# Attention and two MLPs on one core: the work beside attention ordered by a model of the transfers, and casts moved to GpSimd

## The chip, the cores and the metric

One core of a Trainium2 chip runs the whole program. The metric is the device time of one execution in microseconds. Engines are named as in the profile: PE (TensorE), PEld (its weight loads), DVE (VectorE), ACT (ScalarE), POOL (GpSimd), SP (SyncE, which issues nearly all DMAs; its queue is SPq).

## What is computed

Sigmoid attention over 48 heads, then two MLPs, one behind the other, on the 1792 rows that come out:

```python
scores = q @ k.T / sqrt(64) - log(448)          # (4, 12, 448, 64) each, float32
x = (1 / (1 + exp(-scores))) @ v                # then heads side by side: (1792, 768)
h = x @ w_in;   x = where(h > 0, h, exp(min(h, 0)) - 1) @ w_out     # 768 -> 2048 -> 768
h = x @ w_in2;  return (h - tanh(h)) @ w_out2                       # 768 -> 2048 -> 768
```

The four weight matrices arrive as 8-byte floats and are narrowed to float32 on the chip.

## The kernel before

**Attention.** The 48 heads are 24 pairs. A pair's queries and keys are loaded (L222, and 64 rows of keys and values that don't fill a tile by L234 and L242), set side by side by POOL (L226), transposed by PE (L312 to L316) into one bank, copied out by DVE or ACT (`to_plain`, L327 and L329), and split in two parts for exact products: `hi` (L335, a cast) and `lo` (L339, what the cast lost). PE then makes scores (L358, L369), ACT the sigmoids (L375, L379), PE the products with the values (L387, L397), and DVE copies the result into the raw tiles R0a to R1b (`xdone`, L408). Two pairs are one round.

**Work beside attention.** While PE does attention, the other engines prepare what follows. Four blocks of the first `w_in` (L580, L582) and all 16 of the first `w_out` (L649, 768 KB each, tiles XB and XA) are loaded; each is narrowed in three steps, one on ACT (L598) and two on DVE (L601, L605); four sums of `w_out`'s parts are made (`p_sum`, L658) and all parts stored to DRAM (L663). From round six on the raw tiles are split into operands of the first product: `x_sum` (L759), `x_head` (L769, a cast on ACT), `x_rest` (L775, on DVE). There are 21 heads of operands for the first 1024 tokens and 21 for the other 768, each 128x512 or 128x384.

**The products.** Each MLP is two products, with Strassen's seven multiplications; PE runs them group by group (L803, then L958). One group of the first product is seven multiplications for each of the two parts of the tokens. ACT and DVE make its weights (L732, L735; POOL the sums of weights, L718) and take its results (L815 and on).

**What sets the order.** `Sched` holds operations with an engine, a cost, what they wait for and a rank. Attention alone is planned first (ranks from `PHASES`, a 12 us `ROUND` for two pairs); then everything is placed in one list by start time, and each engine's instructions stand in its queue in that order. An operation that isn't attention's is put on ACT or DVE only where it ends before the next planned one is due, give or take `GIVE`. A transfer counts as landed a fixed latency after its issue (2.5 to 12 us), however many are under way. Ranks of the side work are set by `fixed`: a block of `w_out` every 12 us.

```python
if k not in plan and planned.get(queue) and c[0] + ops[k][1] > plan[planned[queue][-1]] + late + GIVE:
    c = (10 ** 9,) + c[1:]
```

Of the kernel before, what the change touches and what calls it, by code (L numbers as in the profile page):

```python
# [16 lines left out]
class Sched:  # L17
# [3 lines left out]
    def __init__(self):  # L21
        self.ops, self.before, self.plan = {}, {}, {}
# [7 lines left out]

    def emit(self, only_plan=False):
        ops, plan, late = self.ops, self.plan, 0

        planned = {q: sorted((k for k in plan if ops[k][0] == q), key=plan.get, reverse=True) for q in ("ACT", "DVE")}
# [12 lines left out]
        while any(ready.values()):  # L47
            best = None
            for queue, keys in ready.items():
                t0 = free.get(queue, 0)  # L50
                for k, t in keys.items():
                    c = (max(t, t0), ops[k][4], str(k))
                    if k not in plan and planned.get(queue) and c[0] + ops[k][1] > plan[planned[queue][-1]] + late + GIVE:
                        c = (10 ** 9,) + c[1:]
                    if best is None or c < best[0]:
                        best = c, queue, k
# [8 lines left out]
            done[k] = free[queue] + ops[k][5]  # L65
            order.append((start, len(order), ops[k][2], k))
# [16 lines left out]
GIVE = 100  # L83

# [5 lines left out]
    "t": (2000 - ROUND, 2900 - ROUND), "plain": (2950 - ROUND, 4100 - ROUND), "hi": (4100 - ROUND, 5800 - ROUND), "lo": (4700 - ROUND, 6400 - ROUND),  # L90
    "side": (4500 - 2 * ROUND, 6000 - 2 * ROUND), "ldqk": (7000 - 3 * ROUND, 8500 - 3 * ROUND),
# [7 lines left out]
def kernel(  # L99
# [67 lines left out]
    with tc.manual_schedule():  # L167
# [7 lines left out]
        def attention():  # L175
# [31 lines left out]
            vrest = [vs_p.tile([128, NR, D], F32, name=f"vrest{i}") for i in range(2)]  # L207
# [31 lines left out]
            def ld_vr(g):  # L239
                for z in range(2):  # L240
                    for x in range(2):
                        nc.sync.dma_start(  # L242
                            out=vrest[g % 2][RS * z:RS * z + RS].rearrange("p (i x) d -> x p i d", x=2)[x],
                            in_=rests(1, g).rearrange("(i x h) p d -> x h p i d", x=2, h=2)[x, z ^ x],
                        )
# [27 lines left out]
            def loads(m):  # L273
# [12 lines left out]
                for x, key in enumerate(todo):  # L286
# [4 lines left out]
                    }.get(kind, [])  # L291
                    sch.op(key, "SP", {"ldkr": 2400, "ldvr": 2400}.get(kind, 600), lambda fn=fns[kind], args=args: fn(*args),
# [41 lines left out]
            def hi(n):  # L334
                nc.vector.tensor_copy(out=es[n % 2][:, :EW], in_=kq(n))  # L335
# [27 lines left out]
            def scores_rest(m):  # L363

                ps = buffer("sr", m)
                for x in range(2):
                    for j in range(2):
                        lanes, c = slice(64 * j, 64 * j + 64), 64 * (j ^ x)
# [1165 lines left out]
```

## Time and profile before

| | us |
|---|---|
| median of 3 runs (1009.24 to 1013.07) | 1009.57 |
| the profiled execution | 1009.88 |
| its span, first to last instruction | 1008.2 |
| PE busy, share of the span | 977.1, 97% |
| DVE busy | 780.1, 77% |
| ACT busy | 597.4, 59% |
| POOL busy | 112.1, 11% |

The rows below come from the profile's views: the page's busy times; the table of stretches (per stretch each engine's busy time with its count of instructions, PE's granted clock as a share of full speed, the share of DMA time and the GB/s moved); the timeline of one engine (start, duration, and in brackets the idle time before and what ended it); and groups of instructions by form (count, busy time, mean of one). A stretch from one L369 to another is a whole number of rounds.

### The profile page before, as it was taken

Reading aid. Unit: us, or ns where it says so; the run is one execution under the profiler, and the core shown is the slowest. Engines: PE = TensorE matmul, PEld = TensorE weight load, DVE = VectorE, ACT = ScalarE, POOL = GpSimd, SP = SyncE. Lnnn points to the kernel's source line nnn. Section 1 sums busy time; section 2 is a strip of 40 time slices with the busy share of each in tenths; the row PEclk is TensorE's granted clock in tenths of the full one; section 3 lists DMA queues with packets and bytes.
Section 4 is the critical chain, followed back from the end, with each engine's and each line's share of the span. In section 5 each row is a group of like instructions: output and inputs, shape, how many; then the busy total and the mean of one; then the engine's idle time right before and its main releaser. Section 6 shows DMA issues by size and latency. Waiting matters only on the chain.

```text
span 1008.2 us, 15604 instructions
## 1 busy us (share of the span) xinstructions
PE 977.1 (97%) x5306; PEld 844.7 (84%) x5306; DVE 780.1 (77%) x1143; ACT 597.4 (59%) x943; POOL 112.1 (11%) x110
## 2 busy tenths in 40 slices
PE   8989899689999999999999998999999999999998
PEld 5555455578888888888899997888888999999998
DVE  4879798977888888668887899777777788665673
ACT  4768578756666667665566654444444556446652
POOL 2211220202222220000000201111111000000000
PEclk9989899989999999999999999999999999999999
DMA  7899981066666679999984734455555894455442
GB/s 205 286 299 317 300 300 64 31 186 191 191 191 191 191 241 321 372 401 382 373 284 131 242 97 148 160 196 188 186 192 187 325 330 146 125 169 173 128 148 85
DMA packets 145087, 218.61 MB, mean 217 GB/s; under 512 B 21936, under 2 KB 103408, under 8 KB 144752
## 3 DMA queue, kind: packets, MB, share of 16 engines
q1 hardware_dynamic: 143744, 217.10, 64.6%
q8 instruction: 41, 0.67, 0.3%
q10 hardware_dynamic: 1264, 0.52, 0.2%
q14 instruction: 38, 0.31, 0.1%
HBM read 142.61 MB, written 74.97 MB: 216 GB/s over the span
## 4 chain that ended last, share of the span: by engine, by line
PE 90%; DMA 4%; DVE 2%; ACT 1%; issue 1%; SPq 0%; ACTq 0%; DVEq 0%
PE psa L803 13%; PE psd L803 12%; PE psx L803 10%; PE psu L958 7%; PE psv L958 7%; PE psw L958 7%; PE psa L958 6%; PE psb L958 6%; PE psb L803 5%; PE psy L958 5%; PE sps L358 4%; PE pvps L387 4%; PE psx L958 3%; PE psd L958 1%; DMA XB<-in_moe_w_out_dram 1%; DMA vl<-in_v_dram 1%
## 5 line engine op out<-in xcount | busy, mean ns | idle before, releaser
L930 ACT ACTIVATE XB<-t 128x384 fp32r<-128x384 f32 (+1 forms) x111 | 62.0, 562 | 37.5 <-PE psw L958 9.9
L718 POOL TENSOR_TENSOR second<-second 128x384 f32<-128x384 f32 x15 | 19.2, 1279 | 552.1 <-DMA t<-x_forms 213.5
L934 DVE TENSOR_TENSOR XB<-t,XB 128x384 fp32r<-128x384 f32 (+1 forms) x111 | 68.3, 626 | 11.4 <-ACT XB L930 11.1
L379 ACT ACTIVATE an<-sps,bias 128x896 f32<-128x896 f32 x72 | 68.6, 1008 | 3.7 <-PE pvps L387 2.0
L358 PE MATMUL sps<-e 64*128 64x448 f32 x432 | 55.1, 395 | 9.7 <-ACT ar L375 9.3
L358 PEld LDWEIGHTS sps<-e 64*128 64x128 f32 x432 | 40.3, 197 | 25.1 <-ACT ar L375 10.5
L930 ACT ACTIVATE XB<-spare 128x512 fp32r<-128x512 f32 (+1 forms) x72 | 41.1, 573 | 27.0 <-PE psw L958 11.2
L387 PE MATMUL pvps<-an,vl 128*64 128x448 f32 x288 | 56.8, 543 | 0.0
L803 PE MATMUL psa<-XB,W 128*128 128x512 f32 x192 | 54.6, 393 | 0.0
L934 DVE TENSOR_TENSOR XB<-spare,XB 128x512 fp32r<-128x512 f32 (+1 forms) x72 | 44.2, 622 | 8.0 <-ACT XB L930 7.7
L958 PE MATMUL psu<-XB,XB 128*128 128x384 f32 (+1 forms) x192 | 46.3, 348 | 0.0
L226 POOL COPY first<-raw_qk 128x384 f32<-128x384 f32 (+1 forms) x44 | 34.2, 798 | 109.1 <-DMA raw_qk<-in_k_dram 79.5
L958 PE MATMUL psv<-XB,XB 128*128 128x384 f32 (+1 forms) x192 | 46.1, 348 | 0.0
L958 PE MATMUL psw<-XB,XB 128*128 128x384 f32 (+1 forms) x192 | 46.1, 348 | 0.0
L387 PEld LDWEIGHTS pvps<-an,vl 128*64 128x64 f32 x288 | 19.6, 137 | 31.6 <-issue 29.1
L803 PEld LDWEIGHTS psa<-XB,W 128*128 128x128 f32 x192 | 36.4, 190 | 7.7
L832 ACT ACTIVATE spare<-t 128x512 f32<-128x512 f32 (+1 forms) x33 | 19.0, 579 | 36.9 <-DVE t L820 35.9
L718 POOL TENSOR_TENSOR first<-first,second 128x384 f32<-128x384 f32 x30 | 40.1, 1336 | 1.2
L803 PE MATMUL psd<-XB,W 128*128 128x512 f32 x144 | 37.0, 401 | 1.5 <-DVE W L735 1.3
L836 ACT ACTIVATE spare<-spare 128x512 f32<-128x512 f32 (+1 forms) x64 | 36.6, 572 | 0.7
L958 PE MATMUL psa<-XB,XB 128*128 128x384 f32 (+1 forms) x156 | 36.8, 347 | 0.0
L958 PE MATMUL psb<-XB,XB 128*128 128x384 f32 (+1 forms) x156 | 36.8, 347 | 0.0
(362 smaller groups left out, 2732.6 us busy)
## 6 DMA issues: line engine op xcount, KB each, us to landing
x_forms<-R1b SPq DMA_DIRECT2D x58, 256.0 KB, 2.0
first<-p_forms SPq DMA_DIRECT2D x36, 384.0 KB, 6.3
t<-x_forms SPq DMA_DIRECT2D x64, 192.0 KB, 2.9
t<-x_forms SPq DMA_DIRECT2D x47, 256.0 KB, 4.9
x_forms<-t SPq DMA_DIRECT2D x44, 256.0 KB, 2.0
x_forms<-R1b SPq DMA_DIRECT2D x58, 192.0 KB, 4.7
spare<-x_forms SPq DMA_DIRECT2D x36, 256.0 KB, 4.7
x_forms<-t SPq DMA_DIRECT2D x44, 192.0 KB, 3.4
```

Of the source, the lines that this page charges most:

```text
L226: nc.gpsimd.tensor_copy(out=(ql, kl)[w][:, n % NL].rearrange("p c (h d) -> p c h d", h=2), in_=x)
L358: nc.tensor.matmul(out=ps[:, j, :S], lhsT=e[lanes, EW * kz + u * 128:EW * kz + (u + 1) * 128], rhs=e[lanes, EW * qz + KW:EW * qz + EW], st ...
L379: nc.scalar.activation(out=a, in_=T.pop(("s", n, u))[:, :, :S], func=ACTF.Sigmoid, bias=bias, scale=scale)
L387: nc.tensor.matmul(out=T["o", m][D * j:D * j + D, j ^ x, :S], lhsT=vl[m % NVL][:, x, 3 * j + u], rhs=a[:, j], start=(u == 0), stop=False,)
L718: by.tensor_tensor(out=out, in0=x, in1=y, op=op)
L803: nc.tensor.matmul(out=ps, lhsT=w[wz][:, k0:k0 + 128], rhs=xs[xz][:, kk], start=(opens and n == 0), stop=(n == 3 * KH - 1), skip_group_che ...
L832: nc.scalar.activation(out=r, in_=h, func=ACTF.Tanh)
L836: nc.scalar.activation(out=r, in_=r, func=ACTF.Exp, scale=-1.0)
L930: nc.scalar.activation(out=at_place(og_place[i, s, p, j], 0, i)[:, :HW[s]], in_=T["graw", i, s, p, j], func=ACTF.Copy)
L934: nc.vector.tensor_tensor(out=lo, in0=T.pop(("graw", i, s, p, j)), in1=f(hi), op=ALU.subtract)
L958: nc.tensor.matmul(out=T["o2", tag], lhsT=lhsT, rhs=rhs, start=(p in OPENS and j == 0 and x == 0), stop=(j == NG - 1 and x == 2), skip_gro ...
```

## The change

It does six things.

1. `Sched.moves` gives each DMA a time on one pipe that all transfers share; a load counts as landed when the pipe has come to it.
2. `latest()` works out how late each planned operation of attention on ACT, DVE and POOL may start; side work may now delay it by 0.6 (`SLACK`) of that. POOL becomes a planned queue.
3. `hi` of pairs 2 to 23 moves from DVE to POOL, `x_head` of the first 1024 tokens (21 casts, 128x512) from ACT to POOL, and `x_sum` T3 and T4 of the other tokens (6 subtractions, 128x384) from DVE to POOL.
4. The heads of a pair keep their natural order: `pv` writes both heads of a pair to one bank, `scores_rest` and `pv_rest` use the four quarters of PE in another assignment, so the first `w_in` is loaded by one DMA a block where three stood.
5. The rows of `vrest` are laid out for that order, in four DMAs as before.
6. `fixed` paces the side work anew (a block of `w_out` every 14 us from the start, of `w_in` every 12 us), and `PHASES` moves `hi`, `lo`, `side` and `ldqk` a little.

```diff
-        planned = {q: sorted((k for k in plan if ops[k][0] == q), key=plan.get, reverse=True) for q in ("ACT", "DVE")}
+        planned = {q: sorted((k for k in plan if ops[k][0] == q), key=plan.get, reverse=True) for q in ("ACT", "DVE", "POOL")}
+        limit = self.latest() if plan else {}
...
-                    if k not in plan and planned.get(queue) and c[0] + ops[k][1] > plan[planned[queue][-1]] + late + GIVE:
+                    if k not in plan and planned.get(queue) and c[0] + ops[k][1] > limit[planned[queue][-1]] + late + GIVE:
...
+            if k in self.moves:
+                moved = max(moved, start + 1400) + self.moves[k]
+                done[k] = moved + 600
...
+    def latest(self):
...
+            if queue in ("PE", "SP"):
+                found[k] = plan[k]
+            else:
+                by = [found[u] - cost - latency for u in users[k]]
+                if queue in last:
+                    by.append(last[queue] - cost)
+                found[k] = max(plan[k], min(by, default=plan[k]))
+                last[queue] = found[k]
+        return {k: plan[k] + SLACK * (t - plan[k]) for k, t in found.items()}
...
-                nc.vector.tensor_copy(out=es[n % 2][:, :EW], in_=kq(n))
+                (nc.gpsimd if n > 1 else nc.vector).tensor_copy(out=es[n % 2][:, :EW], in_=kq(n))
...
-                        out=T["o", m][D * j:D * j + D, j ^ x, :S], lhsT=vl[m % NVL][:, x, 3 * j + u], rhs=a[:, j], start=(u == 0), stop=False,
+                        out=T["o", m][D * j:D * j + D, x, :S], lhsT=vl[m % NVL][:, x, 3 * j + u], rhs=a[:, j], start=(u == 0), stop=False,
...
-                        lanes = slice(64 * (j ^ x), 64 * (j ^ x) + 64)
+                        lanes = slice(64 * x, 64 * x + 64)
...
             def sums_on(i, s, x):
-                return "DVE"
+                return "POOL" if (i, s) == (0, 1) and x in ("T3","T4") else "DVE"
...
             def heads_on(i, s):
-                return "ACT"
+                return "ACT" if i or s else "POOL"
...
+                sch.moves["load", n] = 2700 if live and wide else 1100
...
-                    fixed[done] = 3 * CYCLE + n
+                    fixed[done] = n * ROUND
...
-                    fixed[k] = (2 * k[1] + 2) * CYCLE
+                    fixed[k] = 2 * k[1] * PACE
```

**What moves in the queues.** Line numbers differ between the two programs: L598 becomes L614, L375 L402, L379 L406, L649 L665, L663 L679, L222 L249, L718 L734.

On SP, around the load of the third block of `w_in` (R1a). Its narrowing on ACT stands in both programs right before the fifth `ar`. Before, from the loads of queries and keys of pairs 10 and 11 (`raw_qk`) to those of pairs 12 and 13:

```order
L222 DMA raw_qk<-in_q_dram 112x2x256
L663 DMA p_forms<-XB_71 128x4x384
L259 DMA vl_119<-in_v_dram 128x4x192
L663 DMA p_forms<-XB_71 128x384
L242 DMA vrest_117<-in_v_dram 64x2x64 x4
L580 DMA R1a<-in_moe_w_in_dram 64x6x256
L582 DMA R1a<-in_moe_w_in_dram 64x3x256 x2
L234 DMA krest_116<-in_k_dram 64x2x64 x4
L663 DMA p_forms<-XB_71 128x2x384
L222 DMA raw_qk<-in_k_dram 128x2x192
```

Now, up to the loads of pairs 10 and 11 and the values behind them:

```order
L665 DMA XB_71<-in_moe_w_out_dram 128x1536
L603 DMA R1a<-in_moe_w_in_dram 128x6x256
L249 DMA raw_qk<-in_k_dram 128x2x192
L249 DMA raw_qk<-in_q_dram 112x2x256
L249 DMA raw_qk<-in_k_dram 128x2x192
L679 DMA p_forms<-XB_71 128x384
L249 DMA raw_qk<-in_q_dram 112x2x256
L285 DMA vl_119<-in_v_dram 128x4x192
L269 DMA vrest_117<-in_v_dram 64x2x64 x4
```

The third block is now one DMA where three stood, and it is issued ahead of the loads of pairs 10 and 11 and of all that stood between these and its old place.

On ACT, around the eighth `ar` (sigmoids of the rest rows); `an` are the other sigmoids, XB<-XB and XB<-XA narrowing steps of `w_out`, XA<-R0a and XA<-R0b operand heads. Before:

```order
L375 ACTIVATE ar<-sps,bias 128x896
L379 ACTIVATE an<-sps,bias 128x896 x3
L327 ACTIVATE plain_122<-sps 128x832
L379 ACTIVATE an<-sps,bias 128x896 x3
L598 ACTIVATE XB_71<-XA_70 128x768 x2
L769 ACTIVATE XA<-R0b 128x512 x2
L375 ACTIVATE ar<-sps,bias 128x896
```

Now:

```order
L402 ACTIVATE ar<-sps,bias 128x896
L406 ACTIVATE an<-sps,bias 128x896 x3
L354 ACTIVATE plain_122<-sps 128x832
L614 ACTIVATE XB_71<-XB_71 128x768
L406 ACTIVATE an<-sps,bias 128x896 x3
L614 ACTIVATE XB_71<-XA_70 128x768
L402 ACTIVATE ar<-sps,bias 128x896
```

The two narrowing steps of one block of XA stood together before the sigmoids; now one stands there, another is between sigmoids, and the operand heads are gone from ACT.

On POOL, from the last round of attention into the first product. Before:

```order
L226 COPY first<-raw_qk 128x384
L226 COPY first<-raw_qk 112x512
L718 TENSOR_TENSOR second<-second 128x384
L718 TENSOR_TENSOR first<-first,second 128x384
L718 TENSOR_TENSOR second<-second,first 128x384
L718 TENSOR_TENSOR first<-first,second 128x384
```

Now:

```order
L783 CAST XA_1526<-R0b 128x512 x3
L362 CAST e_83<-plain_121 128x832
L362 CAST e_123<-plain_122 128x832
L783 CAST XB_1622<-R0a 128x512 x6
L783 CAST XB_1622<-R0b 128x512 x3
L734 TENSOR_TENSOR second<-second 128x384
L734 TENSOR_TENSOR first<-first,second 128x384
L734 TENSOR_TENSOR second<-second,first 128x384
L775 TENSOR_TENSOR R1a<-R1a 128x384 x3
L775 TENSOR_TENSOR R1b<-R1b,R1a 128x384 x3
L734 TENSOR_TENSOR first<-first,second 128x384
```

The `hi` casts (L362) and the operand heads (L783) have joined POOL's queue, and the sums T3 and T4 (L775) stand behind three of the four sums of the second group's weights (L734).

## Rows read from the trace of the kernel before

**Rows 1.** The page, part 1: engine, busy us, share, instructions.

```profile
PE 977.1 (97%) x5306; PEld 844.7 (84%) x5306; DVE 780.1 (77%) x1143; ACT 597.4 (59%) x943; POOL 112.1 (11%) x110
```

**Rows 2.** Stretches: from:to, length, PE, PEld, DVE, ACT, POOL, clock, DMA share, GB/s.

```profile
0.00:24.47 24.47, 21.27 (x121) 13.69 (x125) 10.24 (x13) 11.36 (x13) 5.51 (x13) 1.00 0.75 198
24.47:60.67 36.20, 36.20 (x278) 20.55 (x274) 31.03 (x41) 28.05 (x31) 9.99 (x13) 1.00 0.93 304
60.67:123.86 63.19, 53.84 (x369) 31.31 (x365) 48.46 (x70) 41.09 (x48) 12.69 (x16) 0.89 0.94 301
123.86:171.23 47.37, 47.32 (x353) 25.62 (x346) 43.41 (x67) 37.40 (x46) 6.68 (x8) 1.00 0.61 206
171.23:209.70 38.47, 27.26 (x122) 23.06 (x119) 36.71 (x64) 25.07 (x48) 5.30 (x4) 0.91 0.14 52
209.70:235.09 25.39, 25.39 (x127) 22.82 (x127) 20.63 (x31) 15.49 (x28) 5.81 (x4) 1.00 0.63 198
```

**Rows 3.** Timeline of PE at the three longest of its waits.

```profile
66.90 1.49 PE L358 MATMUL sps<-e 64*128 64x448 f32 x6 [3.89 <-ACT ar L375]
...
111.55 1.49 PE L358 MATMUL sps<-e 64*128 64x448 f32 x6 [4.73 <-ACT ar L375]
...
204.46 1.01 PE L803 MATMUL psd<-XB,R0a 128*128 128x384 f32 x2 [7.21 <-ACT R1b L815]
```

**Rows 4.** Timeline of ACT ahead of the first two of them.

```profile
65.06 0.89 ACT L598 ACTIVATE R1b<-R1a 128x768 f32<-128x768 f32 x1 [6.43 <-DMA R1a<-in_moe_w_in_dram]
...
105.81 0.90 ACT L598 ACTIVATE XB<-XA 128x768 f32<-128x768 f32 x1 [4.71 <-DMA XA<-in_moe_w_out_dram]
108.68 0.89 ACT L598 ACTIVATE XB<-XA 128x768 f32<-128x768 f32 x1 [1.97 <-DMA XA<-in_moe_w_out_dram]
109.47 1.13 ACT L769 ACTIVATE XA<-R0b 128x512 fp32r<-128x512 f32 x2
```

**Rows 5.** Timeline of SP's queue: the issue of the loads that ACT waited for.

```profile
58.38 0.59 SPq L580 DMA_DIRECT2D R1a<-in_moe_w_in_dram  x1
59.70 1.76 SPq L582 DMA_DIRECT2D R1a<-in_moe_w_in_dram  x2
...
98.91 0.88 SPq L649 DMA_DIRECT2D XA<-in_moe_w_out_dram  x2
```

**Rows 6.** Groups of DVE by form, up to 209.7 us (busy us, mean ns).

```profile
L339 DVE TENSOR_TENSOR e<-plain,e 128x832 fp32r<-128x832 f32 x24 | 27.3, 1136 | 0.8
L658 DVE TENSOR_TENSOR XB<-XB 128x384 f32<-128x384 f32 x32 | 18.4, 613 | 0.0
...
L335 DVE CAST e<-plain 128x832 fp32r<-128x832 f32 x24 | 16.4, 684 | 2.5 <-PE sps L358 1.0 <-ACT plain L327 1.0
...
L601 DVE TENSOR_SCALAR XB<-XB 128x768 int32<-128x768 int32 x16 | 10.0, 623 | 4.0 <-ACT XB L598 4.0
```

**Rows 7.** Timeline of DVE where POOL is idle beside it.

```profile
38.74 0.55 DVE L601 TENSOR_SCALAR XB<-XB 128x768 int32<-128x768 int32 x1
39.21 0.55 DVE L658 TENSOR_TENSOR XB<-XB 128x384 f32<-128x384 f32 x1
...
41.71 0.59 DVE L335 CAST e<-plain 128x832 fp32r<-128x832 f32 x1
42.34 1.02 DVE L339 TENSOR_TENSOR e<-plain,e 128x832 fp32r<-128x832 f32 x1
```

**Rows 8.** Timeline of POOL: one copy of each form where DVE leaves it alone.

```profile
21.55 0.51 POOL L226 COPY first<-raw_qk 128x384 f32<-128x384 f32 x1 [6.32 <-DMA raw_qk<-in_k_dram]
...
24.73 0.61 POOL L226 COPY first<-raw_qk 112x512 f32<-112x512 f32 x1 [0.46 <-PE pvps L397]
```

**Rows 9.** Groups of POOL by form, whole span.

```profile
L226 POOL COPY first<-raw_qk 112x512 f32<-112x512 f32 x22 | 19.4, 880 | 3.7 <-DMA raw_qk<-in_q_dram 2.3 <-PE pvps L397 0.5 <-PE sps L316 0.5
L718 POOL TENSOR_TENSOR second<-second 128x384 f32<-128x384 f32 x15 | 19.2, 1279 | 552.1 <-DMA t<-x_forms 213.5 <-DVE second L605 194.0 <-ACT t L815 62.9
```

**Rows 10.** Timeline of PE in an undisturbed round: products of 64 rows or 64 columns.

```profile
37.42 2.09 PE L358 MATMUL sps<-e 64*128 64x448 f32 x18
...
43.15 4.73 PE L387 MATMUL pvps<-an,vl 128*64 128x448 f32 x24
```

More of the change, by code (lines that the diff above doesn't have):

```diff
@@ L21, in __init__ @@
     def __init__(self):
-        self.ops, self.before, self.plan = {}, {}, {}
+        self.ops, self.before, self.plan, self.moves = {}, {}, {}, {}
     def op(self, key, queue, cost, fn, after, rank, latency=60):
@@ L83 @@
 GIVE = 100
+SLACK = 0.6
+PACE = 7000
 ROUND = 2 * CYCLE
@@ L206, in attention @@
             krest = [ld_p.tile([128, 2, DD], F32, name=f"krest{i}") for i in range(2)]
-            vrest = [vs_p.tile([128, NR, D], F32, name=f"vrest{i}") for i in range(2)]
+            vrest = [vs_p.tile([128, NR // 2, 2, D], F32, name=f"vrest{i}") for i in range(2)]
             heads = [x.rearrange("b h s d -> (b h) s d") for x in (k, v)]
@@ L239, in ld_vr @@
             def ld_vr(g):
[L240 to L245, printed above, removed]
+                for y in range(NR):
+                    i, x = divmod(y, 2)
+                    nc.sync.dma_start(
+                        out=vrest[g % 2][RS * x:RS * x + RS, i], in_=rests(1, g)[2 * y:2 * y + 2].rearrange("h p d -> p h d")
+                    )
             def ld_first(kind, i):
@@ L291, in loads @@
                     }.get(kind, [])
+                    sch.moves[key] = {"ldv": 650 * (args[-1] - args[-2]) if kind == "ldv" else 0, "ldkr": 570, "ldvr": 570, "ldkfirst": 630, "ldqfirst": 740}[kind]
                     sch.op(key, "SP", {"ldkr": 2400, "ldvr": 2400}.get(kind, 600), lambda fn=fns[kind], args=args: fn(*args),
@@ L395, in pv_rest @@
                     for j in range(2):
-                        lanes = slice(64 * (j ^ x), 64 * (j ^ x) + 64)
+                        lanes = slice(64 * x, 64 * x + 64)
                         nc.tensor.matmul(
-                            out=T["o", m][D * j:D * j + D, j ^ x, :S], lhsT=vrest[n // NR % 2][lanes, n % NR], rhs=a[lanes, j], start=False, stop=True,
+                            out=T["o", m][D * j:D * j + D, x, :S], lhsT=vrest[n // NR % 2][lanes, m % (NR // 2), j], rhs=a[lanes, j], start=False, stop=True,
                         )
@@ L442, in attention @@
                     op(("plain", n, y), by, int(1.06 * (c1 - c0)) + 120 if by == "DVE" else int(0.87 * (c1 - c0)) + 190, to_plain, [("t", n), ("sr", m - 1), ("lo", n - 2)])
-                op(("hi", n), "DVE", 600, hi, copied(n) + [("s", n - 2, u) for u in range(3)])
+                op(("hi", n), *(("POOL", 1100) if n > 1 else ("DVE", 600)), hi, copied(n) + [("s", n - 2, u) for u in range(3)])
                 op(("lo", n), "DVE", 1020, lo, [("hi", n)])
@@ L1115, in job @@
                     kept_by[key] = n
+                    if place == 4:
+                        fixed["keep", n, key] = n * ROUND + 3
+                    sch.moves["keep", n, key] = 1100
                     raw_op(("keep", n, key), "SP", 600, lambda: keep(n, key), [done], 12000 if place == 4 else 5600)
@@ L1203, in operands @@
                             n_y = n // len(parts_)
[L1204 removed]
+                            raw_op(("x_head",) + key + (str(y),), by, act(n_y) if by == "ACT" else int(1.05 * n_y) + 120,
                                    lambda x=x, y=y: x_head(i, s, x, y), need + was)
@@ L1439, in mlp @@
                 stored = [] if j < 2 else [("p_store", j - 2, 2)]
+                sch.moves.update({("p_store", j, c): (540, 1080, 2160)[c] for c in range(3)})
                 for c in range(2):
-                    op("p_load", (j, c), "SP", 600, p_load, [("s", 1, 0)] + (was[c:c + 1] if wide else held), 11000)
+                    sch.moves["p_load", j, c] = 2150
+                    paced = (2 * j + c) * PACE // CYCLE
+                    op("p_load", (j, c), "SP", 600, p_load, ([("s", paced, 0)] if paced else [("t", 1)]) + (was[c:c + 1] if wide else held), 11000)
                     done = ("p_load", j, c)
```

35 lines of the change are left out of this document (17 added, 18 removed).

## The prediction

> **What bounds the kernel now.** The page comes first: PE is busy 977.1 of 1008.2 us, no other engine above 780 [rows 1]. So a gain can only come from the 31 us in which PE is idle, and from stretches at a low clock. The table of stretches shows where these are. Three rounds of attention that nothing disturbs take 36.20 us, 12.07 each, at full clock; the next stretch holds four rounds and takes 63.19 [rows 2]. Four rounds at 12.07 would be 48.3, so 14.9 us are lost there. The first group of the first product takes 38.47 us, the second, with the same multiplications, 25.39 [rows 2]: another 13.1. In both stretches the granted clock is 0.89 and 0.91, everywhere else 1.00 [rows 2]: behind each wait PE works for some microseconds at 1.2 GHz instead of 2.4, which is in the sums. Together 28.0 us; the changed kernel can't end much before 1009.9 - 28.0 = 981.9, since PE has the same work in the same time in all else.
>
> Who is waited for, the timelines show. PE's long waits in attention, 3.89 and 4.73 us, end with a sigmoid on ACT, the third, 7.21 us in the product, with ACT's copy of a result [rows 3]. In attention ACT isn't overworked: it stands still for 6.43 us ahead of a narrowing step, until the third block of `w_in` lands, and for 4.71 and 1.97 us ahead of two steps of `w_out` [rows 4]. The sigmoids are queued behind. That load was issued from 58.38 to 61.5 us by three DMAs, hardly before ACT came to the step; the two of `w_out` went out at 98.9 and landed 7 and 10 us later, with the DMA engines 0.94 busy [rows 4, 5]. In the product DVE is the bound: 36.71 of 38.47 us busy [rows 2]; ACT's copies, and PE behind them, wait for slots that DVE frees late.
>
> **The transfers, as one pipe.** The third block's load now stands ahead of the loads of pairs 10 and 11, one round and some ten DMAs earlier, and is one DMA, which issues in about 0.6 us (the row of 0.59) where three took over 3 [rows 5]. The paired steps of `w_out` are spread between sigmoids. For the waits to go, loads must be about 8 us earlier against ACT (6.43, and 4.71 + 1.97 in the other case); a round is 12. I take all of the 14.9 us off here, as far as DVE permits (next part). Bounds: nothing, if the pipe is later by as much as the issue is earlier, and 14.9. The bytes are the same, and attention gets shorter: at 304 GB/s and 0.93 of the DMA time in an undisturbed round [rows 2], loads stay the resource with the least slack, which the last rival takes up.
>
> **The casts.** Each part on each engine:
> - DVE loses 22 `hi` at 684 ns, 15.0 us, and six sums, at the 0.55 us of a subtraction of that size 3.3 us [rows 6, 7].
> - ACT loses 21 operand heads; two of them take 1.13 us [rows 4], so some 12 us. ACT's idle time absorbs what is left; no gain by itself.
> - POOL gains 22 casts of 832 columns. Copies take 0.51 and 0.61 us for 384 and 512 columns alone [rows 8], on that line 0.88 for 832; by the mean of a crowded copy (880 against 610 ns, [rows 8, 9]) 1.27. The 21 heads take 0.61 to 0.88, the six sums 1.28 each by the sums of weights [rows 9]. Alone, 19.4 + 12.8 + 7.7 = 39.9 us. POOL was busy 40 us up to 209.7 us [rows 2] and has room.
>
> **What POOL costs DVE.** Operations of DVE are longer beside POOL. Against their time alone (1.02, 0.59, 0.55, 0.55 us) the means are 1.136, 0.684, 0.613, 0.623 [rows 6, 7]: 24 x 0.116 + 24 x 0.094 + 32 x 0.063 + 16 x 0.073 = 8.2 us. POOL's 44 copies alone would be 22 x (0.51 + 0.61) = 24.6 us. So each microsecond of POOL's work costs DVE 0.33 in these four kinds; with those not counted I take 0.4, between nothing and 1.0 (POOL's work blocks DVE for all its length). The 39.9 us then cost DVE 16.0.
>
> The Trainium skill, SBUF — State Buffer, section "SBUF: two separate sides", says that DVE and GpSimd share one pair of ports by an exclusive lock, held for the whole instruction, and that the loser fully blocks. By that rule alone the price could be the 1.0; the rows show 0.33 to 0.4, since half the time POOL is the one that waits. By the rule's end the sum below comes to 1014, by the rows to 990.
>
> **The sum, on DVE.** Up to 209.7 us DVE is busy 10.24 + 31.03 + 48.46 + 43.41 + 36.71 = 169.9 us and idle 14.2, 5.2, 14.7, 4.0 and 1.8 in the five stretches [rows 2]. The 14.7 are the stalls of ACT and go. The 14.2 (nothing has been loaded yet) and the 5.2 stay. Of the last 5.8 I keep half, as DVE will more often find work waiting. Work: 169.9 - 15.0 - 3.3 + 16.0 = 167.6. So the first group ends at 167.6 + 14.2 + 5.2 + 2.9 = 189.9 us instead of 209.7: DVE, not PE (181.7), sets that point. The gain is 19.8 us. From there on PE runs at 25.39 us a group without idle time [rows 2], and the rest only moves forward. 1009.9 - 19.8 = 990.1; say **990**. The profiled execution, 1009.88, is the median within 0.3 us. The uncertain terms are the idle time kept (up to 5.8) and the factor of 0.4 (0.25 to 0.55 is 10 to 22 us): 984 to 997.
>
> **Edits that cost nothing.** The blocks of `w_in`: fewer DMAs, same bytes; behind attention SP's work is covered by 0.14 to 0.63 of DMA time [rows 2]. The rows of `vrest` come by four DMAs as before. The new quarters of PE: products of two row halves (L358, 18 in 2.09 us) and of two column halves (L387, 24 in 4.73 us) stand in one round already [rows 10], so the change brings no kind of sharing that isn't there. If the four quarters no longer ran together, L369 and L397 would double: 8 passes each in a round, at the 0.1 us that one of L358's takes, 1.6 us a round and 19 us in 12 rounds; that is the upper end. There is no gain, the passes being the same. I take 0. T3 and T4 stand behind three sums of the next group's weights on POOL, which wait for a load; three sums and three subtractions are 7.7 us, against 25 us of a group; PE waits for them only if these start later than some 15 us into the group. `hi` stands on POOL behind copies that wait for loads, but those copies feed the transposes ahead of it, so it adds no load to wait for; the longer cast, at worst 0.7 us more, fits ahead of scores that come most of a round later.
>
> **The rivals.**
> 1. *PE alone is the bound, 982* (981 to 984). The factor is under 0.2, or DVE's order lets PE go on while DVE is late. For it: a few tenths of the factor decide, and some of DVE's work ahead of 189.9 us belongs to the second group and can be late. Against: DVE is 36.71 of 38.47 us busy in the product [rows 2]. 0.18.
> 2. *POOL blocks DVE, 1002* (997 to 1016). The factor is 0.7 to 1.0: 28 to 40 us on DVE, the group ends at 202 to 214. DVE is then late in attention too, and PE waits for `lo`. For it: DVE's queue gets denser, and so collisions with POOL more likely, than in the rows that gave 0.33. 0.14, of which under half below 1004.8. (The lock of the Trainium skill's SBUF — State Buffer, "SBUF: two separate sides", would do this if DVE were always the loser; the rows bear out a third of it.)
> 3. *ACT still waits for loads, 1017* (1004 to 1030): slower. Twenty blocks have a first narrowing step in ACT's queue ahead of sigmoids. Today two places in it stop PE, for 14.9 us with the slow clock behind them, 7 each. The new pace asks for the same 44 MB or so (some 300 GB/s over 150 us, [rows 2]) in 15 us less, with the first blocks earlier, and a load that ACT finds late stops all of attention. From four such stops on, 28 us, what is lost exceeds today's 14.9 and the 13.1 of the product; at five, 35 us, with 7 us of the product won by DVE's idle time, it is 1009.9 + 20 - 13 = 1017. For it: landings of 7 to 10 us [rows 4, 5]. Against: most loads stand a round ahead of their use now, ACT has 8 us of idle time in three rounds [rows 2] and can wait 2 us in each unpunished. 0.07.
> 4. *The new quarters don't run together, 1009*: 990 and 19 us. 0.03.
>
> **How the numbers follow.** The forecast has 0.58, the rivals 0.18, 0.14, 0.07 and 0.03. A change under 0.5%, 5 us, is about what a measurement of this kernel can't tell from none. Faster than 1004.8: 0.58 + 0.18 + 0.06 of the second = 0.82. Between 1004.8 and 1014.9: 0.06 of the second, 0.02 of the third, 0.02 of the fourth = 0.10. Slower: the rest, 0.08. The range 981 to 1004 holds the forecast, the first rival and the lower part of the second; 0.18 are outside.
>
> **What would show it.** Right: four rounds of attention in 48 to 51 us wherever one looks, ACT's waits for `R1a` and `XA` down from 13.1 us to under 4; the first group 27 to 33 us long; DVE over 0.93 busy from 60 us to its end; POOL's casts of 832 columns at 0.9 to 1.3 us; and every later group at 25.39. Wrong: waits of ACT for a load before a sigmoid, of over 3 us (the third rival); PE waiting for `lo`, or casts over 1.5 us and `x_rest` well over 0.7 (the second); L397 and L369 at twice their time (the fourth); or a loss behind the first group, which no step here foresees.

## The result, and the profile after

The change is slower: 1023.7 us, median of 4 runs (1022.44 to 1024.83), against 1009.4 (1008.63 to 1013.07, 4 runs): ratio 1.0134, interval 1.0106 to 1.0162. The forecast was 990.0, range 981 to 1004.

The page of the changed kernel, part 1, answers to [rows 1]:

```profile
PE 978.5 (96%) x5306; PEld 839.5 (82%) x5306; DVE 795.8 (78%) x1115; ACT 580.4 (57%) x922; POOL 181.2 (18%) x159
```

The work has moved as planned: POOL has 69 us more, ACT 17 less. But DVE, which was to lose 18.3 us, has 15.7 more: 2.8 of these stand up to the end of the first group (172.7 against 169.9 us, the sums of its column in the first five stretches), 12.9 behind it. Now the table of stretches, with the columns of [rows 2] and cut at the same multiplications (start, three rounds, four rounds, four rounds and the end of attention, first group, second group):

```profile
0.00:23.73 23.73, 20.17 (x124) 12.86 (x128) 7.40 (x9) 10.67 (x13) 7.53 (x16) 0.93 0.73 201
23.73:62.83 39.10, 36.51 (x281) 20.56 (x277) 33.47 (x44) 29.51 (x33) 19.48 (x16) 1.00 0.95 313
62.83:113.67 50.84, 48.33 (x372) 27.42 (x368) 49.23 (x58) 34.71 (x39) 32.16 (x34) 1.00 1.02 341
113.67:167.16 53.49, 49.11 (x354) 26.97 (x346) 52.71 (x70) 35.15 (x42) 31.84 (x29) 0.97 0.57 193
167.16:200.47 33.31, 27.29 (x121) 23.77 (x118) 29.85 (x46) 19.91 (x39) 16.57 (x10) 0.90 0.18 65
200.47:226.75 26.28, 25.66 (x127) 22.77 (x127) 21.99 (x31) 15.62 (x28) 5.22 (x4) 1.00 0.56 192
```

The four rounds that took 63.19 us take 50.84, and the first group 33.31 instead of 38.47. Against that, the first three rounds are 2.9 us longer and the last four 6.1. The first group ends at 200.47 us instead of 209.7: 9.2 us won, not 19.8. The last row is the first of a new kind: the second group takes 26.28 us. Four of the five groups behind it:

```profile
226.75:253.36 26.61, 25.70 (x128) 22.81 (x127) 21.48 (x30) 15.77 (x29) 5.22 (x4) 1.00 0.52 177
253.36:281.07 27.71, 25.93 (x128) 22.73 (x127) 21.47 (x30) 15.72 (x29) 5.20 (x4) 1.00 0.52 178
281.07:308.95 27.88, 25.96 (x128) 22.72 (x127) 21.47 (x30) 15.75 (x29) 5.20 (x4) 1.00 0.51 173
308.95:336.21 27.26, 25.96 (x128) 22.72 (x127) 21.48 (x30) 15.74 (x29) 5.22 (x4) 1.00 0.51 176
```

and two of them in the kernel before:

```profile
235.01:260.41 25.40, 25.40 (x128) 22.82 (x127) 20.28 (x31) 15.89 (x28) 5.81 (x4) 1.00 0.59 185
285.81:311.21 25.40, 25.40 (x128) 22.82 (x127) 20.41 (x31) 15.95 (x28) 5.81 (x4) 1.00 0.60 189
```

No engine is full there (DVE 21.5 of 27.7 us), the clock is 1.00, and still a group is up to 2.5 us longer. Comparing the start of the same multiplication in both traces, after minus before: end of the first group -9.2 us, end of the seventh +2.0, end of the first MLP +6.1, end of the second +14.8. So 24.0 us are lost behind the first group.

The waits of the changed kernel between 210 and 370 us (engine and line waiting, what for, us in total, times, longest) name the place:

```profile
DVE first L617 <- ACT first L614: 20.0, 11, 3.3
...
ACT first L614 <- DMA first<-in_moe_w_in_dram: 10.3, 5, 2.2
ACT first L614 <- DMA second<-in_moe_w_in_dram: 10.1, 6, 2.3
...
PE psd L819 <- ACT t L831: 3.6, 4, 1.1
...
PE psa L819 <- DVE t L836: 2.4, 3, 0.9
```

In the kernel before, in that window, ACT waits 0.5 us for these loads and PE for nothing at all. One instance, in ACT's timeline of the changed kernel, and the two issues in SP's:

```profile
285.82 0.52 ACT L852 ACTIVATE spare<-spare 128x384 f32<-128x384 f32 x1
288.46 0.89 ACT L614 ACTIVATE first<-first 128x768 f32<-128x768 f32 x1 [2.13 <-DMA first<-in_moe_w_in_dram]
289.26 0.59 ACT L831 ACTIVATE t<-psd 128x512 f32<-128x512 f32 x1
...
294.10 0.89 ACT L614 ACTIVATE first<-second 128x768 f32<-128x768 f32 x1 [2.32 <-DMA second<-in_moe_w_in_dram]
296.21 0.63 ACT L846 ACTIVATE spare<-spare 128x512 f32<-128x512 f32 x1 [1.22 <-DVE spare L836]
```
```profile
283.15 0.38 SPq L603 DMA_DIRECT2D first<-in_moe_w_in_dram  x1
...
286.54 0.38 SPq L603 DMA_DIRECT2D second<-in_moe_w_in_dram  x1
```

The load goes out at 283.15, the narrowing step is due at 286.3 and stands until 288.46, when the block has landed; the copies of results (L831), for which PE waits, stand behind it. The page's part 6 gives the landings (KB each, median us from issue):

```profile
first<-in_moe_w_in_dram SPq DMA_DIRECT2D x14, 768.0 KB, 5.3
second<-in_moe_w_in_dram SPq DMA_DIRECT2D x14, 768.0 KB, 6.7
...
R1b<-in_moe_w_out_dram SPq DMA_DIRECT2D x8, 768.0 KB, 7.1
```

With nothing else in its pipe, the planner now counts such a load as landed 1400 + 2700 + 600 = 4700 ns after its start; before the change it counted 600 + 8500 = 9100. The change's line `sch.moves["load", n] = 2700 if live and wide else 1100` stands in `job()`, which makes the blocks of attention's idle time (place 4) and those of the MLPs alike. That is **theory A**: the price is for attention, but it also moved the MLPs' narrowing steps ahead of their loads. **Rival B**: the loss comes from the single transfers of `w_in`, or from POOL's new work.

### The profile page after: what moved, and what is told of

Its sections match the earlier page's. It is cut to its first block, busy times and chain, and to the rows that moved or that the text cites. A ratio compares the mean times of both kernels' runs of the same rounds, so it can differ in the third digit from the quotient of the medians.

```text
span 1022.7 us, 15569 instructions
## 1 busy us (share of the span) xinstructions
PE 978.5 (96%) x5306; PEld 839.5 (82%) x5306; DVE 795.8 (78%) x1115; ACT 580.4 (57%) x922; POOL 181.2 (18%) x159
## 4 chain that ended last, share of the span: by engine, by line
PE 56%; DVE 17%; DMA 15%; issue 6%; ACT 3%; POOL 2%; SPq 1%; DVEq 0%; ACTq 0%; POOLq 0%
PE psa L819 6%; PE psx L819 6%; PE psd L819 6%; PE psu L974 5%; PE psv L974 5%; PE psw L974 5%; PE psa L974 4%; PE psb L974 4%; DMA second<-in_moe_w_in_dram 3%; PE psy L974 3%; PE psx L974 3%; DVE R1b L881 2%; PE psb L819 2%; DMA vl<-in_v_dram 2%; PE pvps L414 2%
## 5 line engine op out<-in xcount | busy, mean ns | idle before, releaser
L734 POOL TENSOR_TENSOR second<-second 128x384 f32<-128x384 f32 x15 | 20.9, 1396 | 528.3 <-DVE second L621 296.5
L406 ACT ACTIVATE an<-sps,bias 128x896 f32<-128x896 f32 x72 | 67.9, 1011 | 1.5 <-PE pvps L414 0.7
L385 PE MATMUL sps<-e 64*128 64x448 f32 x432 | 53.0, 385 | 1.9 <-ACT ar L402 1.6
L617 DVE TENSOR_SCALAR first<-first 128x768 int32<-128x768 int32 x28 | 15.6, 559 | 41.4 <-ACT first L614 41.4
L253 POOL COPY first<-raw_qk 128x384 f32<-128x384 f32 (+1 forms) x44 | 41.8, 983 | 16.8 <-DMA raw_qk<-in_k_dram 16.0
L734 POOL TENSOR_TENSOR first<-first,second 128x384 f32<-128x384 f32 x30 | 41.1, 1370 | 1.1
L819 PE MATMUL psd<-XB,R0a 128*128 128x384 f32 x96 | 26.9, 362 | 12.5 <-ACT R1b L831 7.8
L819 PE MATMUL psa<-XB,e 128*128 128x512 f32 x96 | 30.9, 403 | 7.7 <-DVE t L836 5.5
L362 POOL CAST e<-plain 128x832 fp32r<-128x832 f32 x22 | 29.2, 1339 | 47.8 <-DVE plain L356 43.7
L366 DVE TENSOR_TENSOR e<-plain,e 128x832 fp32r<-128x832 f32 x24 | 32.4, 1353 | 6.7 <-POOL e L362 6.6
```

Source lines behind the costliest of these rows:

```text
L253: nc.gpsimd.tensor_copy(out=(ql, kl)[w][:, n % NL].rearrange("p c (h d) -> p c h d", h=2), in_=x)
L362: (nc.gpsimd if n > 1 else nc.vector).tensor_copy(out=es[n % 2][:, :EW], in_=kq(n))
L366: nc.vector.tensor_tensor(out=e[:, EW:2 * EW], in0=kq(n), in1=f(e[:, :EW]), op=ALU.subtract)
L385: nc.tensor.matmul(out=ps[:, j, :S], lhsT=e[lanes, EW * kz + u * 128:EW * kz + (u + 1) * 128], rhs=e[lanes, EW * qz + KW:EW * qz + EW], st ...
L406: nc.scalar.activation(out=a, in_=T.pop(("s", n, u))[:, :, :S], func=ACTF.Sigmoid, bias=bias, scale=scale)
L734: by.tensor_tensor(out=out, in0=x, in1=y, op=op)
```

## The experiments

Medians of one kernel repeat within 2 to 4 us, so differences under 3 us are not read. The kernel before had 1008.0, 1010.6 and 1008.6 us beside the three sets below; where runs of two sets are compared, their ratios to the kernel before give differences up to 2.5 us away from those of the medians. Each edit lets the planner run again, so that some order beside the edit moves with it.

### The loss behind the first group

**The pipe for attention's blocks only** (in the change):

```diff
-                sch.moves["load", n] = 2700 if live and wide else 1100
+                if place == 4:
+                    sch.moves["load", n] = 2700 if live and wide else 1100
...
-                    sch.moves["keep", n, key] = 1100
+                    if place == 4:
+                        sch.moves["keep", n, key] = 1100
```

> The change, but with the pipe's entries for the weight blocks (both for their loads and for keeping them) only where a block belongs to attention's idle time; the blocks of the two MLPs go back to the fixed latency, the casts and the three-into-one load of w_in stay. Theory A (the short landing time, 2700 ns after the pipe's 1400, was given to all loads; behind attention it puts the narrowing activation on ScalarE some 2 us before its block has landed, and ScalarE's snaps and so TensorE wait behind it): the 24 us lost behind the first group of the first MLP go, the 9.2 us won up to there stay, so 998 to 1003 us, and the waits of the narrowing for loads of w_in between 210 and 370 us, 20.4 us in all, fall under 4. Rival B (the loss behind attention comes from the new form of the w_in loads, from the sums on GpSimd or from the later start of the blocks): 1020 to 1025 us.

Measured 998.9 us (998.15 to 1000.8), ratio to before 0.9908 [0.9884, 0.9932]. Groups again take 25.40 us:

```profile
225.28:250.68 25.40, 25.40 (x128) 22.82 (x127) 20.41 (x31) 15.94 (x28) 5.81 (x4) 1.00 0.55 190
```

The waits of the narrowing for `w_in` between 210 and 370 us are gone, and from the first group to the start of the second MLP each multiplication starts the same 9.7 us before its twin of the kernel before. The same block in ACT's timeline and SP's:

```profile
286.68 0.88 ACT L614 ACTIVATE first<-first 128x768 f32<-128x768 f32 x1
```
```profile
278.39 0.38 SPq L603 DMA_DIRECT2D first<-in_moe_w_in_dram  x1
```

It goes out 2.3 us into its group (276.08), where the change's goes out 2.1 us into its own (281.07); but ACT comes to the step 8.3 us after the issue instead of 3.2. So not the loads moved, the step did. Theory A holds, and rival B falls here already: the single transfers of `w_in` and POOL's new work are all still in this run.

**That part alone, in the kernel before:** the pipe, with its prices for loading and storing the MLPs' blocks and nothing else.

```diff
+            if k in self.moves:
+                moved = max(moved, start + 1400) + self.moves[k]
+                done[k] = moved + 600
...
+                if place != 4:
+                    sch.moves["load", n] = 2700 if live and wide else 1100
...
+                    if place != 4:
+                        sch.moves["keep", n, key] = 1100
```

> The kernel before, and one part of the change alone: the pipe with the short landing times for the weight blocks of the two MLPs and nothing else, so attention and its first group stay as they were. Theory A: it loses what the change lost behind the first group, about 24 us: 1025 to 1037 us, with ScalarE's narrowing waiting for loads of w_in between 210 and 370 us as in the change. Rival B: 1007 to 1012 us.

Measured 1047.9 us, ratio 1.0383 [1.0350, 1.0417]. The part alone makes a slow kernel of a good one, and up to the end of attention nothing moved (first group from 171 to 209.7 us as before). It lost 40 us, not the 24 expected. Its waits between 210 and 370 us:

```profile
ACT first L601 <- DMA first<-in_moe_w_in_dram: 20.6, 6, 3.7
ACT first L601 <- DMA second<-in_moe_w_in_dram: 12.7, 6, 2.9
```

33.3 us where the change has 20.4: here a block still comes in three transfers. For a block of `first` these take 6.4 us from the first issue to the last landing (212.02 to 218.41 in this trace), and the change's single transfer 5.1 (202.80 to 207.93).

**The change with three transfers a block** (the removed branch of `load` put back; half of the rows of these weights then come in another order, so that the products have the same shapes and other values):

> The change, with the first MLP's w_in blocks loaded again by three transfers each instead of one. Rival B in its first form (the single transfer lands later than the three, and the narrowing waits for it): the loss of about 11 us in the rest of the first product goes, 1010 to 1015 us. Theory A: the three land no sooner than the one, the loss stays, 1020 to 1028 us.

Measured 1042.3 us (1041.72 to 1044.07). Rival B's first form falls here too: three transfers are not the remedy, they cost 18.6 us more. Theory A's size is missed as well, as in the run above, where the last of three lands later than the one.

**The change with a longer price:**

```diff
-                sch.moves["load", n] = 2700 if live and wide else 1100
+                sch.moves["load", n] = (2700 if place == 4 else 4500) if live and wide else 1100
```

> The change with one number altered: the weight loads of the MLPs take 4500 ns in the pipe instead of 2700, so that a block counts as landed 6.5 us after its issue, about the medians that the trace shows (5.3 and 6.7 us), and not 4.7. Theory A: the loss behind the first group shrinks from 24 us to between 2 and 12: 1002 to 1012 us. Rival B: 1020 to 1025 us.

Measured 1008.0 us (10 runs, 1006.48 to 1009.97). One number in the planner takes back 15.7 of the 24.8 us between the change and the run with attention's prices alone. A group takes 25.60 us. Most of the 9 us that stay lost are in the second MLP: against the run with attention's prices alone, multiplications start 1.4 us later at its beginning and 10.5 at its end. No weight load is waited for there any more; between 590 and 830 us PE waits 6.5 us for DVE's weights `W` (L751), 1.3 in the other run, as DVE's queue has another order. Whether the prices that this run keeps (1100 for storing and for stored blocks) make that order stays open.

### What the casts are worth

**`hi` back on DVE** (attention's prices only, as in the first run):

```diff
-                (nc.gpsimd if n > 1 else nc.vector).tensor_copy(out=es[n % 2][:, :EW], in_=kq(n))
+                nc.vector.tensor_copy(out=es[n % 2][:, :EW], in_=kq(n))
```

> As the run with the pipe's entries for attention's blocks only, and the first casts of queries and keys (hi) back on VectorE. Over the whole program the change took 18.3 us of work from VectorE at the durations of undisturbed instructions, and VectorE's busy time rose by 15.7 us while GpSimd's rose by 69.1: about 0.49 us of VectorE per us of GpSimd. Theory A with that price: these 22 casts took 29.5 us on GpSimd and so cost VectorE 14.5 us while they save it 12.1, so this run is 0 to 4 us faster than the run with them on GpSimd. Rival C (the price of the prediction, 0.4 or less): this run is 2 to 8 us slower. In both, the share of attention in TensorE's idle time tells the same.

Measured 995.5 us (994.35 to 997.55), ratio 0.9870 [0.9849, 0.9892]: 3.5 us faster than with the casts on POOL, and the ranges don't meet. The last four rounds of attention show it, 48.89 us here and 53.53 with `hi` on POOL. The groups by form of the run with `hi` on POOL, then of this one, say why:

```profile
L366 DVE TENSOR_TENSOR e<-plain,e 128x832 fp32r<-128x832 f32 x24 | 32.8, 1369 | 6.5 <-POOL e L362 6.4
L362 POOL CAST e<-plain 128x832 fp32r<-128x832 f32 x22 | 29.4, 1347 | 46.2 <-DVE plain L356 43.3 <-PE sps L385 2.9
```
```profile
L366 DVE TENSOR_TENSOR e<-plain,e 128x832 fp32r<-128x832 f32 x24 | 27.8, 1160 | 0.4
...
L362 DVE CAST e<-plain 128x832 fp32r<-128x832 f32 x24 | 16.1, 672 | 1.2 <-ACT plain L354 0.8 <-PE sps L385 0.2
```

A cast of 672 ns on DVE became one of 1347 on POOL, `lo` went from 1160 to 1369, and DVE stood 6.5 us at `lo`, the next in its queue, until POOL had done. As an account of the two runs: DVE loses 22 x 0.672 = 14.8 us of casts; its busy time falls by only 2.9 (786.8 to 783.9), so POOL's company cost it 11.9, or 0.61 for each of the 19.4 us that these casts take alone; with 6.1 us more of standing at `lo`, DVE is 3.2 us worse off. The difference in time is 3.5. (How the two parts share it rests on this account; no run takes away one of them alone. Up to the end of the first group DVE's busy time falls by only 1.7, from 175.8 to 174.1, and the price is 0.68; it is 0.64 in the two runs below that have heads and sums back, 167.1 and 164.8.) PE feels it where its transposes wait for DVE's copies into the raw tiles (`xdone`, now L435), 8.2 us between 24 and 165 us with `hi` on POOL:

```profile
PE sps L339 <- DVE R1a L435: 3.8, 2, 2.5
PE sps L339 <- DVE R1b L435: 3.4, 2, 2.1
...
PE sps L339 <- DVE R0b L435: 1.0, 1, 1.0
```

With `hi` on DVE these waits are 2.8 us.

**Heads and sums back on ACT and DVE**, once with `hi` on POOL and once with all casts back, which leaves the pipe and the slack (with the single transfers of `w_in`):

```diff
-                return "POOL" if (i, s) == (0, 1) and x in ("T3","T4") else "DVE"
+                return "DVE"
...
-                return "ACT" if i or s else "POOL"
+                return "ACT"
```

> The change with the pipe's entries for attention's blocks only, and the heads of the first group's operands back on ScalarE, its two sums T3 and T4 back on VectorE; the casts hi stay on GpSimd. Theory D (a us of GpSimd beside VectorE costs VectorE 0.49 us, and VectorE, full from 160 to 195 us, sets the first group's end): heads and sums take about 29 us on GpSimd and cost VectorE 14, against 3.3 us that the sums save it, so this is up to 8 us faster than with them on GpSimd (998.9): 991 to 999 us. Rival C (the prediction's own price, 0.4 or less, and a ScalarE that is late with the heads, 12 us of work): 1001 to 1008 us.

Measured 998.5 us (997.27 to 1001.02), beside 998.9: no difference. That is the upper edge of what D allows, and C's loss is not there.

> The order of work from the pipe and the slack alone: all casts and sums where they were before the change, the pipe's entries for attention's blocks only. Theory D: at least as fast as with the casts on GpSimd, 987 to 996 us, with GpSimd's casts of queries and keys side by side back at about 0.8 us. Rival C: the first group loses its 13 us of stalls again and hi its place beside VectorE's work, 1000 to 1006 us.

Measured 995.7 us (994.12 to 998.48), ratio 0.9847 [0.9828, 0.9867]. All of the gain is there without any cast on POOL: 13 to 17 us by the interval. Its stretches from the first three rounds to the end of the first group:

```profile
24.57:64.13 39.56, 37.03 (x281) 20.39 (x277) 36.35 (x50) 28.23 (x32) 10.69 (x12) 1.00 0.90 297
64.13:115.78 51.65, 49.06 (x372) 27.24 (x368) 47.05 (x67) 39.18 (x47) 13.22 (x16) 1.00 0.97 322
115.78:168.28 52.50, 49.12 (x354) 26.90 (x346) 45.34 (x73) 40.31 (x51) 7.55 (x8) 0.97 0.64 208
168.28:199.70 31.42, 25.79 (x121) 22.94 (x118) 29.25 (x53) 22.00 (x44) 5.69 (x4) 0.89 0.18 63
```

The four rounds are 11.5 us shorter than in [rows 2], the other rounds 3.4 and 5.1 longer, the first group 7.1 shorter. Heads and sums on POOL bring nothing; `hi` on POOL takes 3.5 back with them there, and 2.8, too little to read, without (998.5 against 995.7; in these two traces the first group ends alike, at 199.3 and 199.7 us).

**POOL's copies twice:**

```diff
-                nc.gpsimd.tensor_copy(out=(ql, kl)[w][:, n % NL].rearrange("p c (h d) -> p c h d", h=2), in_=x)
+                for _ in range(2):
+                    nc.gpsimd.tensor_copy(out=(ql, kl)[w][:, n % NL].rearrange("p c (h d) -> p c h d", h=2), in_=x)
```

> The run with hi back on VectorE (995.5 us), and each of GpSimd's 44 copies that lay queries and keys side by side done twice: a doubled suspected cost, with nothing else on VectorE. Alone the second copies are 44 x 0.56 = 25 us of GpSimd, beside VectorE some 37. Theory D (0.49 us of VectorE for each): VectorE's busy time in attention grows by 12 to 18 us, and as it is 9.8 to 10 of 10 there from 60 to 160 us, the end moves by 6 to 16 us: 1001 to 1012 us. Rival E (GpSimd's work costs VectorE nothing; what hi costs on GpSimd is its own longer time in the chain from transposes to scores): 994 to 998 us, VectorE's busy time within 3 us.

Measured 1004.6 us (1002.34 to 1005.23), 9.1 us more. The stretch from 0 to the end of the first group, first in the run without, then in the run with the second copies:

```profile
0.00:194.97 194.97, 180.31 (x1223) 109.56 (x1224) 175.78 (x246) 130.12 (x164) 71.48 (x81) 0.97 0.73 240
```
```profile
0.00:204.00 204.00, 180.55 (x1223) 110.02 (x1224) 184.94 (x246) 130.12 (x164) 111.76 (x125) 0.97 0.70 230
```

DVE has the same 246 instructions and is busy 9.2 us longer, and the stretch is 9.0 longer: here time is DVE's time. 24.6 us of copies alone (44 of those in [rows 8]) cost DVE 9.2, 0.37 for each. Rival E falls; the price for plain copies is near the prediction's 0.33, and theory D's size, 12 to 18 us, was too high for them.

**Half of `hi` on ACT:**

```diff
-                nc.vector.tensor_copy(out=es[n % 2][:, :EW], in_=kq(n))
+                if n % 2:
+                    nc.scalar.activation(out=es[n % 2][:, :EW], in_=kq(n), func=ACTF.Copy)
+                else:
+                    nc.vector.tensor_copy(out=es[n % 2][:, :EW], in_=kq(n))
```

> The run with hi back on VectorE (995.5 us), and the casts of every second pair on ScalarE: 11 casts, 7.4 us less for VectorE, some 10 us more for ScalarE, and none for GpSimd. Theory D (VectorE, full from 60 to 175 us, is the bound, and what the change's casts on GpSimd lost is the price of running beside VectorE): 988 to 994 us. Rival F (what it lost is that lo, the next in VectorE's queue, stands and waits for a cast on another engine, 6.6 us in the change's trace; ScalarE's sigmoids besides wait behind a cast that waits for plain): 996 to 1004 us, with VectorE waiting for ScalarE's cast at lo.

Measured 993.7 us (992.78 to 996.14), ratio 0.9857 [0.9839, 0.9874]: the fastest of all, though its range meets that of `hi` on DVE, and DVE waits 2.3 us at `lo` for ACT's 11 casts. What F names is there, but small; the time is at the upper edge of D's, and 1.8 us are too few to say that it is faster.

**Only the heads back on ACT**, T3 and T4 on POOL (`return "ACT"` in `heads_on`):

> The run with hi back on VectorE (995.5 us), and of the operands' part the heads alone back on ScalarE; the two sums T3 and T4 stay on GpSimd. Theory D (0.49 to 0.65 us of VectorE for each us of GpSimd's work alone): 12.8 us of heads cost VectorE 6 to 8 us in the first group, and ScalarE has room there: 989 to 994 us, the first group 28 to 31 us long instead of 32.9. Rival (ScalarE is as late with the heads as VectorE with its share: a group is no shorter): 995 to 999 us.

Measured 999.2 us, of a wide range (993.91 to 1001.75). Theory D's 989 to 994 is missed, and the first group is 34.95 us long instead of 28 to 31: PE's wait for ACT's copy of a result (L831) in the first group is 8.2 us here and 5.1 with the heads on POOL. That wait, the third of [rows 3], is left in every version but one, 5 to 9 us of it (1.1 in the change with three transfers). What would remove it stays open.

### Two parts that were priced at nothing, or not at all

**Three transfers with the long latency** (`hi` on DVE, attention's prices only):

> The run with hi back on VectorE (995.5 us), where the MLPs' loads have the fixed latency, with the first MLP's w_in blocks again in three transfers (two quarters of their rows come in another order, so the products have other operands of the same size). In the change itself this edit cost 18.6 us. Prediction's step, that one transfer instead of three costs and brings nothing: 994 to 998 us; the 18.6 us were then the short landing time once more, which three transfers miss by further. Rival G (three transfers cost SP's queue its time whatever the planner counts): 1003 to 1015 us.

Measured 1002.1 us (999.4 to 1004.63) beside 995.5. That is nearer to G than to the prediction's step, which falls: one transfer is worth 6.7 us, in attention, where the blocks keep the short price: the two profiled runs are 4.4 us apart, all of it by the end of the first group. Of the waits between 24 and 165 us, with three transfers and with one:

```profile
ACT R1b L626 <- DMA R1a<-in_moe_w_in_dram: 10.1, 3, 3.8
```
```profile
ACT R1b L614 <- DMA R1a<-in_moe_w_in_dram: 4.2, 2, 3.3
```

**No slack** (`SLACK = 0.0`, the rest as there):

> The run with hi back on VectorE (995.5 us), and the slack of planned work set from 0.6 to 0: other work goes ahead of a planned step only if it ends by the step's planned start. If the pipe alone took off attention's stalls, 994 to 999 us and four rounds after the first five in 50 to 52 us as with it; if the slack did a part of it, 1000 to 1008 us, with other work, such as narrowing steps, pushed into the last rounds and the first group.

Measured 999.9 us (999.71 to 1002.52), 4.4 us slower: at the lower end of what a part of the slack would give. Its stretches of the first three rounds and the first group:

```profile
24.63:60.83 36.20, 36.20 (x281) 20.55 (x277) 33.27 (x45) 28.52 (x32) 10.27 (x12) 1.00 0.99 324
...
160.66:202.52 41.86, 28.21 (x121) 23.17 (x118) 40.54 (x60) 22.27 (x42) 14.70 (x12) 0.84 0.14 50
```

Without slack the first three rounds are undisturbed again, 36.20 us as in [rows 2] against 38.24 with it, and attention ends sooner; but the work that it kept out comes in the first group, 41.86 us against 32.94, with DVE full. So the slack is what shortens the first group, by taking its work into attention.

## Why the prediction was wrong

**"From there on PE runs at 25.39 us a group without idle time, and the rest only moves forward."** This step failed, by 24 us. It was read off the row of an undisturbed group [rows 2], that is, off the old order behind attention, and the change also altered the order there. The diff says so: the entry in `moves` is made for every load of `job()`. The 4.7 us that follow from it stand against medians of 5.7 and 6.1 us which the page of the kernel before has for blocks of the same size in the same tiles, the second MLP's (the first's came in three parts, 4.8 to 6.8 us each):

```profile
first<-in_moe_w_in_dram SPq DMA_DIRECT2D x8, 768.0 KB, 5.7
second<-in_moe_w_in_dram SPq DMA_DIRECT2D x8, 768.0 KB, 6.1
```

That comparison was not made. What the runs showed in its place: narrowing steps that wait 20.4 us for their loads in ACT's queue, ahead of the copies that PE needs, and groups of up to 27.88 us. The first, the second and the fourth run above show the cause from three sides: taken out, alone, and by its size.

The price in the code is under all the medians that the trace has for these blocks. The Trainium skill, DMA: Bandwidth & Descriptors, section "Anatomy of one DMA — SWDGE (gpsimd) path", fits 2.0 us and the bytes at 436 GB/s for one DMA from GpSimd's queue, an estimate of 3.8 us for 768 KB. The loads here come from SP's queue and took 5.3 and 6.7 us.

**"The transfers, as one pipe": right where it looked, not for attention as a whole.** The four rounds take 50.84 us (48 to 51 were named), and ACT's waits in attention for `R1a`, `XA` and `XB` fell from 13.1 to 7.5 us (under 4 was named), and PE has no wait over 2.2 us left there. But all other rounds were to stay as they were, and with slack the first three are 1 to 3.4 us longer and the last four 1.5 to 6.2: attention ends 4.1 us earlier in the change, not 14.9, and 3.0 in the run without casts, where ACT still waits 15.7 us for these loads. Without slack (`hi` on DVE) it ends 10.6 earlier and the other rounds keep their length. So the edits without the slack, with the single transfer and the heads on POOL among them, are worth about 10 of the 14.9, and the slack spends a part of that on work that it takes from the first group. That the order without casts brought 13 to 17 us in all, near 14.9, is luck: the first group's 7.1 are in it.

**"The casts" and "What POOL costs DVE": the terms were mis-sized.** The 22 casts were put at 0.88 to 1.27 us and took 1.34 in the changed kernel. The factor of 0.4 is right for plain copies (0.37 with the copies doubled) and too small for `hi` (0.61 to 0.68). Its 0.33 came from four kinds of operations, 72.1 of DVE's 169.9 us; the 0.07 for all others had no row behind it. By the prediction's own sum, DVE's work up to the end of the first group was 172.7 us where 169.9 - 18.3 = 151.6 were to stay: 21.1 for the 39.9 on POOL, or 0.53. The larger mistake is under "Edits that cost nothing": `hi` on POOL was said to fit "ahead of scores that come most of a round later", but `lo` stands behind it in DVE's queue, and DVE waited 6.5 us. So `hi`, put at 15.0 - 0.4 x 19.4 = 7.2 us of gain, cost 3.5 beside the heads on POOL and gained nothing without them. The price of 1.0, which the prediction drew from the lock of the Trainium skill's SBUF — State Buffer, "SBUF: two separate sides", is not what the runs show: 0.37 and 0.61 to 0.68. That section of the Trainium skill ties the lock, on DVE's side, to operations in a two-port mode or with two inputs in SBUF, so it does not give 1.0 for all of DVE's work; no run here sorts DVE's operations by this.

**"The sum, on DVE": DVE sets that point, but the sum was 10.6 us short.** DVE was to be busy 167.6 us and idle 22.3 up to the end of the first group, 189.9; in the changed kernel it is busy 172.7 and idle 27.8, 200.47. With the failed step alone mended, the kernel has 998.9 us: inside the range, and the 9 us to the forecast are this sum's.

**"Edits that cost nothing":** the new quarters of PE do cost nothing (rounds of 36.20 us in the run without slack), which ends the fourth rival. The single transfer of `w_in` was worth 6.7 us.

**The rivals.** The first (PE alone) and the second (POOL blocks DVE) did not decide. The third had the mechanism, a narrowing step that waits for its load in ACT's queue ahead of what PE needs, and a time, 1017, nearer than the forecast's; but it was placed in attention (and its sum takes 13 us of the product off where its text has 7), so that its range holds the measured 1023.7 is luck. The loss happens behind attention, where "a loss behind the first group, which no step here foresees" was the sign to look for.

## What to carry to other kernels

A planner's price acts wherever the key that it is tied to occurs: list all places before counting a stage as unchanged, and hold each price against the landing time that the trace shows for that transfer. Too short a price is worse than too long a one where the consumer stands in an in-order queue ahead of work that the bottleneck needs: 4.4 us less cost 24 us. And work moved off a full engine gains nothing if that engine's next instruction waits for it.

## What the runs showed of the hardware

The company of POOL costs DVE 0.37 us for each microsecond of plain copies and 0.61 to 0.68 for the casts, both counted by the time that POOL needs alone; neither engine always loses. In the changed kernel POOL's sum of weights, 1.0 to 1.7 us elsewhere, once takes 5.01; with `hi` on DVE five of DVE's subtractions, about 0.5 us each alone, take 5.91 together beside three subtractions and a sum on POOL:

```profile
174.07 5.01 POOL L734 TENSOR_TENSOR second<-second 128x384 f32<-128x384 f32 x1 [11.79 <-DMA second<-kept_wi]
```
```profile
177.15 5.91 DVE L791 TENSOR_TENSOR XB<-R1a,XB 128x384 fp32r<-128x384 f32 x5
```
```profile
177.45 3.90 POOL L775 TENSOR_TENSOR R1b<-R1b,R1a 128x384 f32<-128x384 f32 x3
181.32 1.33 POOL L734 TENSOR_TENSOR second<-second,first 128x384 f32<-128x384 f32 x1
```

And a block of 768 KB lands later in three transfers than in one, 6.4 us against 5.1 from the first issue; in a planner with a short price the same bytes cost 18.6 us more.
